# One V load on the SyncE queue: ahead of a transposing DMA instead of behind it

## The chip, the core and the metric

The kernel runs on one core of a Trainium2 chip. Times are device microseconds of one execution. The engines are TensorE (PE, with its weight loads as PEld), VectorE (DVE), ScalarE (ACT), GpSimd (POOL) and SyncE (SP), which here does nothing but issue DMAs.

## The reference

An RWKV-5 attention with a recurrent state, and behind it a feed-forward layer with a SmeLU:

```python
for t in range(S):                      # B, H, S, D = 4, 8, 768, 48
    cur = einsum('bhd,bhe->bhde', u[None] * k[:, :, t], v[:, :, t])
    y[:, :, t] = einsum('bhd,bhde->bhe', r[:, :, t], state + cur)
    state = w[None, :, :, None] * state + einsum('bhd,bhe->bhde', k[:, :, t], v[:, :, t])
x = y.transpose(0, 2, 1, 3).reshape(B * S, H * D)      # 3072 x 384
h = x @ w_in                                           # 384 x 2048
g = where(h >= 1, h, where(h <= -1, 0, (h + 1) ** 2 / 4))
out = g @ w_out                                        # 2048 x 384
```

## The kernel before

The recurrence is worked in chunks of 128 positions. A group is one chunk of two batches; there are 6 chunks by 2 pairs of batches, so 12 groups, numbered 0 to 11. A unit is one batch of a group (group 4 has units 8 and 9). For each group the kernel loads R, K and V in f32 (384 KB each), scales them by powers of w into bf16 (Rs, Ks), transposes these, forms the masked product A of the chunk, multiplies it with V and adds the part from the state: that is y, 128 x 768 in bf16. Its transposed copy xT is the operand of the feed-forward layer, which is worked in four quarters of d_ff: m (matmuls into hp), r, s, g (the SmeLU) and M (matmuls into op), then the copy to o and the store.

The order of all instructions is written out by hand in the table `ORDER`: one word per step, run from left to right, so each engine gets its own steps in that order, and within a queue nothing overtakes. A word is the step's name, the group or unit, `=V`, `=A` or `=G` for the engine and `/` with PSUM banks. Words used below:

- `LR4`, `LK4`, `LV4`: the load of R, K, V of group 4, in `load`, line 253, all issued from SP.
- `V4`: the cast of V32 to bf16 on ScalarE (line 112). The f32 V tiles (`Vi`) have three buffers; loads come in the order LV0, LV1, LV2, LV3, LV5, LV4, LV6, so LV4 writes the buffer that V2 has read.
- `Ks5`, `Rs5`, `KU5`, `RKU5`: scaled products of K and R (line 282), on GpSimd from group 2 on.
- `KT4`, `RT4`: the transposing DMAs of Ks and Rs of group 4 (line 318), from group 4 on, issued from SP.
- `Y8`, `Y9`, `yg4`: the matmuls of y of group 4 (lines 432 and 438), and the addition on VectorE (line 450).
- `xcg3`: the transposing DMA of y of group 3, the fourth group (line 467), from group 3 on, issued from SP.
- `m3.0` to `m3.3`: the four quarters' first matmuls of group 3 (line 475); they read xT. `M3.00` and so on are the second matmuls (line 512).

SP thus carries, in one order, the loads, three kinds of transposing DMAs and the stores. A waiting instruction on SP holds all that stand behind it, also those that wait for nothing.

Of the kernel before, what the change touches and what calls it, by code (L numbers as in the profile page):

```python
# [32 lines left out]
M0.01 g1.0 M1.00/3 M1.10 M1.11 M1.01 Rs2=G s1.2=A g1.2 T5/0 RKU2=G LK4 r1.3=A s1.3=A g1.3 T4/1 LV3 Ks3=G M0.02 M0.03  # L33
LR4 us2 c5=V A5/0 KU3=G Rs3=G c4=V A4/1 AT5 sbf1=A M1.02 M0.12 M0.13 AT4 T6/0 sbf0=A V2 Y4/1 Y5 B2=G og0=A T7/2 c6=A
RKU3=G c7=A yg2 LV5 M1.12 Sp4/0 Sp5 M1.03 X5/2 Tmg2 decayg2=G X4/1 M1.13 A6/0 xc4=A xc5=V m2.0/2 A7/1 us3 AT6 m2.1/0
og1=A LK5 LR5 V3 Y6/3 B3=G sbfg2=A r2.0=A AT7 Y7 m2.2/1 s2.0=A Ks4=G yg3 xcg3 m2.3/3 g2.0 Rs4=G r2.1=A s2.1=A g2.1 LV4
r2.2=A s2.2=A KT4 M2.00/2 M2.10 M2.01 M2.11 r2.3=A KU4=G RT4 RKU4=G g2.2 s2.3=A LK6 m3.0/0 us4 M2.02 m3.1/1 LR6 M2.12
LV6 r3.0 s3.0=A Ks5=G g2.3 M2.03 Sp6/3 Sp7 M2.13 g3.0 m3.2/0 Rs5=G Tmg3 r3.1 s3.1=A RT5 og2=A g3.1 V4 AA4/23 AT9 Ks6=G
r3.2 s3.2=A KT5 m3.3/1 M3.00/3 M3.10 V5 B4=G AT8 Y8/2 Y9 r3.3 g3.2 s3.3=A LK8 M3.11 M3.12 M3.01 M3.02 yg4 AA5/20 g3.3
# [571 lines left out]
```

## Time and profile before

| | us |
|---|---|
| median of three runs | 175.05 (174.41 to 175.17) |
| the profiled execution, its own time | 174.45 |
| its span | 172.7 |
| TensorE's granted clock | 1.0 |

The profile's rows are read like this: a row of the timeline has the start (us from the span's start), the duration, the engine (SPq for SyncE), the line, the operation, what it writes and reads, and how many instructions are merged; a bracket at the end is the engine's idle time before it and what ended it. A DMA's row is only its issue; the time from the start of its issue to its landing stands in the view of DMA issues. The chain of work that ended last is followed back from the last instruction: at each step to what released it, or to the instruction before it on its engine. Matmuls are pipelined and their ends are modelled, so neighbouring rows of TensorE overlap a little.

### The profile page before, as it was taken

The numbers are of one execution on the slowest core, as the hardware profiler recorded it, in microseconds if no ns is written. First come the engines' busy times: TensorE is split into PE (matmuls) and PEld (weight loads), VectorE is DVE, ScalarE is ACT, GpSimd is POOL, SyncE is SP. The second block draws the span as 40 slices with busy tenths as digits, with TensorE's granted clock in tenths as the row PEclk, the third lists the DMA queues.
The fourth block names the chain that finished last, engine by engine and source line by source line (L and its number), as shares of the span: only waits on it lengthen the run. The fifth ranks groups of instructions, "written<-read, shape, count | busy, mean of one in ns | idle before, by whom it ended". The sixth has DMA issues, their size and how long they took to land.

```text
span 172.7 us, 4051 instructions
## 1 busy us (share of the span) xinstructions
PE 164.6 (95%) x1674; PEld 132.8 (77%) x1674; DVE 130.5 (76%) x150; ACT 129.8 (75%) x150; POOL 117.6 (68%) x86
## 2 busy tenths in 40 slices
PE   7989969999999999989999999999999999999991
PEld 5769859866888877588787797696897787888871
DVE  4578798988687788859789779885889958873752
ACT  4355688991699899179979878689695896988940
POOL 3496754998589949999999998999568804300000
PEclk9999999999999999999999999999999999999999
DMA  5999999999995999999999997997999025130022
GB/s 109 193 187 189 200 175 192 222 210 207 176 194 88 212 181 162 193 200 139 201 305 220 185 220 167 209 188 143 294 204 249 4 55 143 39 101 0 8 91 91
DMA packets 103751, 28.26 MB, mean 164 GB/s; under 512 B 98866, under 2 KB 102836, under 8 KB 103732
## 3 DMA queue, kind: packets, MB, share of 16 engines
q1 hardware_dynamic: 101824, 24.75, 79.0%
q0 software_dynamic: 1760, 3.15, 9.9%
q8 instruction: 13, 0.21, 0.6%
q10 hardware_dynamic: 148, 0.10, 0.2%
q14 instruction: 6, 0.05, 0.1%
HBM read 20.45 MB, written 4.72 MB: 146 GB/s over the span
## 4 chain that ended last, share of the span: by engine, by line
PE 88%; ACT 4%; DMA 3%; DVE 2%; issue 1%; POOL 0%; ACTq 0%; DVEq 0%
PE hp L475 35%; PE op L512 34%; PE A L370 3%; PE Y L438 3%; DMA xT<-y 3%; PE Y L432 2%; PE z L566 2%; PE Sp L405 2%; ACT pt L486 1%; PE TK L330 1%; PE T L330 1%; ACT TT L112 1%; PE lwp L207 1%; PE wp L233 1%; PE TR L330 1%; PE up L211 1%
## 5 line engine op out<-in xcount | busy, mean ns | idle before, releaser
L475 PE MATMUL hp<-xT,w_in 128*128 128x256 bf16 x576 | 69.3, 273 | 1.3 <-DMA xT<-y 1.0
L512 PE MATMUL op<-w_out,g 128*128 128x384 bf16 (+1 forms) x400 | 68.5, 320 | 0.0
L498 DVE SCALAR_TENSOR_TENSOR g<-sq,hp 128x1024 bf16<-128x1024 bf16 x48 | 57.9, 1215 | 13.4 <-ACT sq L495 13.4
L475 PEld LDWEIGHTS <-w_in 128*128 128x128 bf16 x576 | 61.9, 114 | 4.8 <-issue 1.6
L486 ACT ACTIVATE pt<-hp 128x1024 f32<-128x1024 f32 x46 | 46.9, 1020 | 13.8 <-PE hp L475 13.8
L512 PEld LDWEIGHTS <-g 128*128 128x128 bf16 x400 | 37.5, 98 | 20.4
L495 ACT ACTIVATE sq<-pt 128x1024 bf16<-128x1024 f32 x46 | 48.3, 1057 | 1.2
L379 DVE TENSOR_TENSOR AT<-A,umask 128x1024 bf16<-128x1024 f32 x20 | 23.7, 1220 | 5.2 <-PE A L370 5.2
L282 POOL TENSOR_TENSOR Ks<-Ki,Wdn 128x768 bf16<-128x768 f32 (+1 forms) x12 | 20.3, 1688 | 8.5 <-DMA Ki<-in_k_dram 4.7
L313 POOL TENSOR_TENSOR V<-Vb,diag 128x768 f32<-128x768 bf16 (+1 forms) x14 | 18.1, 1290 | 9.8 <-DVE diag L304 4.3
L282 POOL TENSOR_TENSOR RKU<-Ri,KU 128x768 f32<-128x768 f32 (+1 forms) x13 | 21.2, 1634 | 1.0 <-DVE KU L282 0.6
L282 POOL TENSOR_TENSOR KU<-Ki,u_sb 128x768 f32<-128x768 f32 (+1 forms) x13 | 21.3, 1636 | 0.5 <-DMA Ki<-in_k_dram 0.5
L416 POOL TENSOR_TENSOR state<-Tm,wCm 128x768 f32<-128x768 f32 x8 | 14.6, 1830 | 9.9 <-DVE Tm L413 9.9
L282 POOL TENSOR_TENSOR Rs<-Ri,Wup 128x768 bf16<-128x768 f32 x10 | 18.3, 1826 | 0.1
L112 ACT CAST Vb<-Vi 128x768 bf16<-128x768 f32 (+1 forms) x14 | 10.2, 733 | 5.9 <-DMA Vi<-in_v_dram 5.8
L450 DVE TENSOR_TENSOR y<-Y,V 128x768 bf16<-128x768 f32 x10 | 9.6, 956 | 5.9 <-PE Y L438 3.3
L304 DVE TENSOR_REDUCE diag<-RKU 128x16 f32<-128x768 f32 (+1 forms) x14 | 11.6, 831 | 1.5 <-POOL RKU L282 1.5
L112 ACT CAST state_bf<-state 128x768 bf16<-128x768 f32 (+1 forms) x12 | 8.5, 717 | 4.2 <-POOL state L416 4.2
L112 ACT COPY o<-op 128x768 f32<-128x768 f32 (+1 forms) x9 | 6.7, 748 | 5.8 <-PE op L512 5.6
L438 PE MATMUL Y<-Vb,AT 128*128 128x48 bf16 x192 | 10.4, 186 | 0.4 <-ACT Vb L112 0.4
L413 DVE TENSOR_TENSOR Tm<-Sp,state 128x768 f32<-128x768 f32 x8 | 7.7, 956 | 3.2 <-PE Sp L405 3.2
L438 PEld LDWEIGHTS <-AT 128*128 128x128 bf16 x192 | 9.5, 98 | 0.7 <-issue 0.5
(73 smaller groups left out, 122.9 us busy)
## 6 DMA issues: line engine op xcount, KB each, us to landing
out_dram<-o SPq DMA_DIRECT2D x11, 384.0 KB, 3.7
Ki<-in_k_dram SPq DMA_DIRECT2D x9, 384.0 KB, 6.1
Ri<-in_r_dram SPq DMA_DIRECT2D x9, 384.0 KB, 6.0
Vi<-in_v_dram SPq DMA_DIRECT2D x9, 384.0 KB, 5.3
Ki<-in_k_dram SPq DMA_DIRECT2D x6, 192.0 KB, 4.0
Ri<-in_r_dram SPq DMA_DIRECT2D x6, 192.0 KB, 4.7
Vi<-in_v_dram SPq DMA_DIRECT2D x6, 192.0 KB, 6.2
w_in<-in_moe_w_in_dram POOLq DMA_DIRECT2D x2, 384.0 KB, 7.7
```

Source lines behind the costliest of these rows:

```text
L112: nc.scalar.copy(out, in_) if e == "A" else engines[e].tensor_copy(out, in_)
L282: engines[e].tensor_mul(part(out)[:, :, :, :D], part(a), rep(b, j1 - j0) if len(b.shape) == 3 and b.shape[1] == H else part(b))
L304: nc.vector.tensor_reduce(d[:, hs], tiles["RKU", g][:, hs, :], AX.X, ALU.add)
L313: engines[e].tensor_mul(t[:, hs, :], tiles["V", g][:, hs, :], tiles["diag", g][:, hs].unsqueeze(2).to_broadcast([P, n, D]))
L379: nc.vector.tensor_mul(t.rearrange("p i n t -> p (i n) t"), tiles["A", n].rearrange("p i (n t) -> p (i n) t", t=P), umask.unsqueeze(1).to_ ...
L416: engines[e].tensor_mul(states[g % BP], tiles["Tm", g], flat(wCm).unsqueeze(1).to_broadcast([P, UNITS, DM]))
L438: nc.tensor.matmul(Y[:, h * D : (h + 1) * D], AT[:, i, p, :], V[:, j * H + h, :], start=(c == 0), stop=True, skip_group_check=True,)
L475: nc.tensor.matmul(hp[:, f, :], w_in_sb[wi][:, i, wo * FG * P + f : (wo + 1) * FG * P : FG], tiles["xT", g][:, :, i, :], start=(i == 0), s ...
L486: nc.scalar.activation(t, tiles["hp", g, q], AF.Relu, bias=0.5, scale=0.5)
L495: nc.scalar.activation(t, p, AF.Square)
L498: nc.vector.scalar_tensor_tensor(out=make("g", ("g", g, q), [P, FG, TOK], BF16), in0=tiles["sq", g, q], scalar=1.0, in1=tiles["hp", g, q], ...
L512: nc.tensor.matmul(tiles[key][:, i, : o1 - o0], tiles["g", g, q][:, f, j * P : (j + 1) * P], w_out_sb[wi][:, wo, f * DO + o0 : f * DO + o1 ...
```

## The change

The word `LV4` moves from behind `g2.1` to ahead of `xcg3`:

```diff
-og1=A LK5 LR5 V3 Y6/3 B3=G sbfg2=A r2.0=A AT7 Y7 m2.2/1 s2.0=A Ks4=G yg3 xcg3 m2.3/3 g2.0 Rs4=G r2.1=A s2.1=A g2.1 LV4
+og1=A LK5 LR5 V3 Y6/3 B3=G sbfg2=A r2.0=A AT7 Y7 m2.2/1 s2.0=A Ks4=G yg3 LV4 xcg3 m2.3/3 g2.0 Rs4=G r2.1=A s2.1=A g2.1
```

Of the words between the two places only `xcg3` is on SP. Here is SyncE's program around that place, with the semaphores that each instruction waits for; the loads at the top are LK5 and LR5, the two transposing DMAs at the bottom KT4 and RT4:

```order
 L253 DMA Ki<-in_k_dram 128x16x48 [waits DMAHW2_49,Pool_49]
 L253 DMA Ri<-in_r_dram 128x16x48 [waits DMAHW3_49,Pool_49]
-L467 DMA_TRANSPOSE xT<-y 128x6x128 [waits DMAHW4_49,DVE_49]
-L253 DMA Vi<-in_v_dram 128x16x48 [waits DMAHW5_49,Activation_49]
+L253 DMA Vi<-in_v_dram 128x16x48 [waits DMAHW5_49,DMAHW4_49,Activation_49]
+L467 DMA_TRANSPOSE xT<-y 128x6x128 [waits DVE_49]
 L318 DMA_TRANSPOSE KT<-Ks 128x8x128 [waits DMAHW6_49,Pool_49]
 L318 DMA_TRANSPOSE RT<-Rs 128x8x128 [waits DMAHW7_49,Pool_49]
```

The two instructions change places. Both take the next of eight DMA semaphores in turn, so they also exchange these; the V load's waits are for earlier DMAs of those semaphores (the halves of V of group 2, which used the same buffer) and for the cast V2.

What stands further behind on SyncE reads the same before and after. These rows are LV6, RT5, KT5, LK8, then the transposing DMA of y of group 4 (xcg4):

```order
L253 DMA Vi<-in_v_dram 128x16x48 [waits DMAHW2_49,Activation_49]
L318 DMA_TRANSPOSE RT<-Rs 128x8x128 [waits DMAHW3_49,Pool_49]
L318 DMA_TRANSPOSE KT<-Ks 128x8x128 [waits DMAHW4_49]
L253 DMA Ki<-in_k_dram 128x16x48 [waits DMAHW5_49]
L467 DMA_TRANSPOSE xT<-y 128x6x128 [waits DMAHW6_49,DVE_49]
```

Nothing moved there; xcg4 is the transposing DMA whose reader is m4.0. TensorE, VectorE, ScalarE and GpSimd keep their programs; only the names of the two exchanged semaphores change in their waits.

## The prediction

> **What bounds the kernel now.** I read the busy times first, then the same by stage, then TensorE's waits, then the chain of work that ended last, and last the rows of the SyncE queue (SP), which the change touches.
>
> ```profile
> span 172.7 us, 4051 instructions
> PE 164.6 (95%) x1674; PEld 132.8 (77%) x1674; DVE 130.5 (76%) x150; ACT 129.8 (75%) x150; POOL 117.6 (68%) x86
> ```
>
> TensorE is the busiest engine by 30 us. The view by stretches says where its idle time lies; its columns are the stretch, its length, and the busy time of PE, PEld, DVE, ACT and POOL.
>
> ```profile
> 54.00:74.00 20.00, 19.16 (x186) 14.23 (x185) 16.36 (x16) 15.49 (x18) 17.47 (x11) 1.00 1.04 176
> 74.00:90.00 16.00, 15.84 (x179) 13.45 (x179) 12.03 (x12) 13.72 (x16) 15.67 (x10) 1.00 1.08 207
> 90.00:164.00 74.00, 74.00 (x747) 60.12 (x745) 57.98 (x55) 61.73 (x66) 45.74 (x27) 1.00 0.74 145
> ```
>
> From 54 to 164 us TensorE idles 0.84 + 0.16 + 0.00 = 1.00 us. TensorE's waits in that stretch are a single row:
>
> ```profile
> PE hp L475 <- DMA xT<-y: 1.0, 1, 1.0
> ```
>
> So behind 54 us one wait, and only that one, can be taken away; after it TensorE runs without a hole to 164 us. The chain shows what it waits for:
>
> ```profile
> 68.71 0.96 DVE y L450
> 69.74 4.38 DMA xT<-y
> 74.16 1.47 PE hp L475 x12
> ```
>
> This is the transposing DMA of the fifth group's y (xcg4): y is done at 68.71 + 0.96 = 69.67, the DMA is issued at 69.74 and lands 4.38 us later, and the first matmul of m4.0 follows at 74.16.
>
> **Why that DMA takes 4.38 us.** The SP queue's rows (start, duration of the issue):
>
> ```profile
> 44.00 1.53 SPq L253 DMA_DIRECT2D Vi<-in_v_dram  x1
> 45.62 1.91 SPq L253 DMA_DIRECT2D Ki<-in_k_dram  x1
> 47.63 2.13 SPq L253 DMA_DIRECT2D Ri<-in_r_dram  x1
> 53.52 1.30 SPq L467 DMA_TRANSPOSE xT<-y  x1
> 54.91 0.53 SPq L253 DMA_DIRECT2D Vi<-in_v_dram  x1
> 55.54 2.48 SPq L318 DMA_TRANSPOSE KT<-Ks  x1
> 58.11 1.26 SPq L318 DMA_TRANSPOSE RT<-Rs  x1
> 59.42 0.58 SPq L253 DMA_DIRECT2D Ki<-in_k_dram  x1
> ...
> 61.61 1.91 SPq L253 DMA_DIRECT2D Vi<-in_v_dram  x1
> 63.62 4.05 SPq L318 DMA_TRANSPOSE RT<-Rs  x1
> 67.71 1.30 SPq L318 DMA_TRANSPOSE KT<-Ks  x1
> 69.07 0.57 SPq L253 DMA_DIRECT2D Ki<-in_k_dram  x1
> 69.74 2.30 SPq L467 DMA_TRANSPOSE xT<-y  x1
> ```
>
> SP stands still from 47.63 + 2.13 = 49.76 to 53.52, waiting for the fourth group's y, and then issues back to back until 72 us. The DMA view gives the times from issue to landing. First the V load at 44.00; then the R load at 47.63, the V load at 54.91 (the one that moves), xcg3 and KT4; then the K load at 69.07, RT5, KT5 and xcg4.
>
> ```profile
> Vi<-in_v_dram SPq DMA_DIRECT2D x1, 384.0 KB, 6.2
> ```
> ```profile
> Ri<-in_r_dram SPq DMA_DIRECT2D x1, 384.0 KB, 6.7
> Vi<-in_v_dram SPq DMA_DIRECT2D x1, 384.0 KB, 4.2
> xT<-y SPq DMA_TRANSPOSE x1, 2.9
> KT<-Ks SPq DMA_TRANSPOSE x1, 4.4
> ```
> ```profile
> Ki<-in_k_dram SPq DMA_DIRECT2D x1, 384.0 KB, 4.3
> RT<-Rs SPq DMA_TRANSPOSE x1, 6.0
> KT<-Ks SPq DMA_TRANSPOSE x1, 2.8
> xT<-y SPq DMA_TRANSPOSE x1, 4.4
> ```
>
> A transposing DMA on an empty queue lands after 2.8 to 2.9 us and its issue takes 1.3; behind loads it takes 4.4 to 6.0, and the issue 2.3 to 4.05. xcg4 stands behind a load issued at 69.07 that itself stands behind everything since 54.91. Meanwhile the DMA engines were idle. These are the shares of 40 slices of 0.25 us from 48 to 58:
>
> ```profile
> DMA  9999999999999999996220000007999115999999
> ```
>
> The hole runs from about 52.6 to 54.7 us: the loads of the fifth group's K and sixth group's R have drained, and SP may not issue what stands behind xcg3.
>
> **The change, part by part.** It moves one instruction, the 384 KB V load (LV4), on one queue; no engine's program is reordered and nothing is added.
>
> *LV4 earlier.* Its buffer is the third group's, whose cast on ScalarE is long done:
>
> ```profile
> 41.56 0.83 ACT L112 CAST Vb<-Vi 128x768 bf16<-128x768 f32 x1 [2.96 <-DMA Vi<-in_v_dram]
> ```
>
> So it is issued at 49.8, for about 2 us like the three loads ahead of it (1.53 to 2.13): SP is free again at 51.9, before y is done. The landings give a load's time on a full queue: 44.00 + 6.2 = 50.2 and 47.63 + 6.7 = 54.3, with two loads' data between: 2.05 us each. LV4 lands at 54.3 + 2.05 = 56.35 instead of 54.91 + 4.2 = 59.1. Nobody waits for it there; its own gain is nothing.
>
> *xcg3 now stands behind a load.* It is issued at 53.52 as before (y sets that). From below it lands at 53.52 + 2.9 = 56.4, as on an empty queue; from above at 53.52 + 6.0 = 59.5, by RT5's row, behind three loads. The nearer rows are those behind one load: the load at 54.91 lands at 59.1 and KT4 at 55.54 + 4.4 = 59.95; the load at 69.07 lands at 73.4 and xcg4 at 74.1. That is 0.7 to 0.85 behind the load, so xcg3 lands at 56.35 + 0.8 = 57.15. Its reader is m3.0:
>
> ```profile
> 54.90 2.76 PE L512 MATMUL op<-w_out,g 128*128 128x384 bf16 x16
> 57.50 1.25 PE L475 MATMUL hp<-xT,w_in 128*128 128x256 bf16 x10
> ```
>
> M2 covers it until 57.50. Cost nothing, with 0.35 us to spare; what goes beyond that is paid in full.
>
> *SP's rows behind it come earlier.* A transposing DMA that stands behind loads lands 1.9 to 2.1 us after its issue ends (KT4: 58.02 to 59.95; RT5: 67.67 to 69.6; xcg4: 72.04 to 74.1). So xcg3's issue ends at about 55.15, and KT4 follows directly, now with no load ahead of it: 1.30, like KT5 behind RT5, instead of 2.48. RT4 adds 1.26 and ends at about 57.8 instead of 59.37. **SP's lead is 1.6 us.** The two loads behind keep it. RT5 also needs Rs5 from GpSimd, and the K load feeds GpSimd's next step:
>
> ```profile
> 60.29 1.82 POOL L282 TENSOR_TENSOR Rs<-Ri,Wup 128x768 bf16<-128x768 f32 x1
> 64.48 1.83 POOL L282 TENSOR_TENSOR Ks<-Ki,Wdn 128x768 bf16<-128x768 f32 x1 [2.38 <-DMA Ki<-in_k_dram]
> ```
>
> Rs5 is done at 62.11, RT5 was issued at 63.62; 1.6 earlier would be 62.0, so that it starts some 0.1 later than the lead allows. That costs nothing, since its 4.05 us are set by the loads draining ahead of it, not by its start: it ends at 66.05. GpSimd's 2.38 us of waiting shrink too, so it falls behind nowhere. KT5 and LK8 follow; LK8 lands at 73.4 - 1.6 = 71.8.
>
> *xcg4.* Still issued at 69.74, because y is set by TensorE. It lands at the later of 69.74 + 2.9 = 72.65 and 71.8 + 0.75 = 72.55. TensorE is ready at 71.69 + 1.48 = 73.17:
>
> ```profile
> 71.69 1.48 PE L512 MATMUL op<-w_out,g 128*128 128x384 bf16 x8
> ```
>
> So the 1.00 us goes entirely, with 0.5 to spare. A lead of 74.1 - 73.17 = 0.95 us is enough for that.
>
> *What is late next.* Behind 74 us the rest moves as one: xcg5 and later ones hang on y, so on TensorE; the loads behind xcg4 are issued about 1 us earlier, since its issue takes 1.30 instead of 2.30; GpSimd has gained more than 1 us; ScalarE waits for TensorE there and can follow:
>
> ```profile
> ACT pt L486 <- PE hp L475: 10.8, 16, 2.1
> ```
>
> **Sum:** 0 (LV4) + 0 (xcg3) - 1.00 (xcg4) = -1.0 us on the profiled execution's own 174.45 us (span 172.7 and 1.75 around it): 173.45. The median of the three runs, 175.05, lies 0.60 above that execution; I take 1.0 off it: **174.05 us**.
>
> **The rivals.**
>
> *The gain comes in part* (174.2 to 174.9, say 174.4). One DMA engine can lag: the shares above fall at 52.6, yet the R load lands at 54.3. RT5, which meets such a lag, ends its issue 0.5 to 0.9 us later than a clean queue would let it. If xcg3 does so, it lands at about 57.7, m3.0 is 0.2 late, and SP's lead is 1.05, just enough: -0.8, 174.25. A lead under 0.95 leaves the difference as a wait. For it: the margins are 0.35 and 0.5 us. Against: each needs tenths beyond my middle. The Trainium skill, "DMA: Bandwidth & Descriptors", section "Queues, rings and completion order", speaks on this side: each DMA engine takes its descriptors in ring order, and a DMA counts as complete only when every engine's part is; the trace agrees (0.8 us behind the load ahead), and by that rule the lag passes on to xcg3.
>
> *The gain is given back* (up to 175.05). TensorE might not be the bound behind 74 us, and catch up with another engine. ScalarE's waits speak against it (10.8 us for TensorE), and so do 74.00 busy of 74.00. The Trainium skill, "Trainium Kernel Development and Optimization", section "Performance Expectations", warns that matmul busy time is a bad metric since matmuls are pipelined, and points to the weight loads: those are busy 60.12 of 74.00 here, which would leave room; the trace's single wait says otherwise, and no run here settles it.
>
> *The change doesn't do what it says* (175.05): LV4 held by its buffer or semaphore until 53.5. The cast at 41.56 and the standing SP speak against it.
>
> *Slower.* xcg3 behind LV4 behaves as RT5 behind three loads: 6.0 us, landing at 59.5, so m3.0 starts 2.0 late. SP is then held for 4.05, to 57.57, and RT4 ends 0.8 later than before. xcg4's wait vanishes under the delay: 2.0 - 1.0 = +1.0, 176.05. It decides from a landing of 58.5 on. For it: R's and K's data are still in flight when LV4 is issued. Against: 3.7 us pass from LV4's issue to xcg3's, against 2.0 between the V load at 61.61 and RT5.
>
> *More than forecast* (173.45): two of three runs took 0.6 to 0.7 us more than the profiled one; if that is a longer wait at the same place, it goes too.
>
> **How the numbers follow.** Forecast 0.50, in part 0.25, given back 0.08, no effect 0.04, slower 0.05, more 0.08. Likeliest: 174.05. The range reaches from "more" to no change with a spread of the runs, 173.4 to 175.1, and leaves out the slower case and the tails. A measurement can tell about 0.5%, 0.88 us, from no change: faster means under 174.17. The forecast lies 0.12 beyond that, so I count 0.40 of its 0.50, all of "more" and a little of "in part": faster 0.50, same 0.45, slower 0.05.
>
> **What would show it.** LV4's issue at 49.8 and its landing near 56.3; xcg3's landing near 57.1 and no wait at m3.0; KT4's issue near 55.2 at 1.3 us; RT4's end near 57.8; GpSimd's wait for K well under 2.38; xcg4's issue at 69.7 with a landing under 73.2; TensorE busy 20.0 of 20.0 from 54 to 74. I am wrong if m3.0 waits for xT, if xcg4 still lands behind 73.2, or if TensorE shows a new wait behind 74.

## The result, and the profile after

| | before | the change |
|---|---|---|
| median of 21 runs each, us | 174.51 (174.03 to 175.81) | 173.41 (173.23 to 175.23) |
| span of the profiled execution, us | 172.7 | 171.5 |

The ratio is 0.9939, with a 95% interval of 0.9920 to 0.9958: faster by 0.6%. In a second, shorter measurement (below) it was 0.9968, 0.9940 to 0.9995. All ratios in this text leave out the few slow runs.

The same stretches as before the change, now of the profile after; the columns are the stretch, its length, and the busy time of PE, PEld, DVE, ACT and POOL:

```profile
54.00:74.00 20.00, 20.00 (x196) 15.16 (x194) 16.29 (x16) 16.28 (x18) 18.61 (x12) 1.00 1.19 187
74.00:90.00 16.00, 16.00 (x183) 13.62 (x181) 13.24 (x13) 14.10 (x15) 15.59 (x10) 1.00 1.00 220
90.00:163.00 73.00, 73.00 (x738) 59.10 (x736) 56.97 (x54) 60.78 (x65) 44.66 (x26) 1.00 0.74 141
```

TensorE is busy for 109.00 of 109.00 us: the hole of 1.00 us is gone, and none has opened behind it. TensorE's timeline after the change, at the first matmuls of m3.0 and of m4.0:

```profile
57.50 1.47 PE L475 MATMUL hp<-xT,w_in 128*128 128x256 bf16 x12
73.00 1.47 PE L475 MATMUL hp<-xT,w_in 128*128 128x256 bf16 x12
```

m3.0 starts where it did before (57.50), m4.0 at 73.00 instead of 74.16. That is 1.16 of the 1.2 us by which the spans differ. The SyncE queue after the change (start, duration of the issue):

```profile
50.05 2.99 SPq L253 DMA_DIRECT2D Vi<-in_v_dram  x1
53.46 1.95 SPq L467 DMA_TRANSPOSE xT<-y  x1
55.51 1.25 SPq L318 DMA_TRANSPOSE KT<-Ks  x1
56.85 1.26 SPq L318 DMA_TRANSPOSE RT<-Rs  x1
...
62.07 3.05 SPq L318 DMA_TRANSPOSE RT<-Rs  x1
65.18 2.40 SPq L318 DMA_TRANSPOSE KT<-Ks  x1
67.63 0.57 SPq L253 DMA_DIRECT2D Ki<-in_k_dram  x1
69.69 1.21 SPq L467 DMA_TRANSPOSE xT<-y  x1
```

LV4 stands in SP's idle time; KT4's issue takes 1.25 instead of 2.48, as no load stands between it and xcg3; and xcg4's takes 1.21 instead of 2.30. The queue is not empty then: LK8, the load ahead of xcg4, lands only at 71.97. But LK8 was issued 2.06 us ahead of xcg4 instead of 0.67, and xcg4 lands 0.63 behind it. The times from issue to landing, in the DMA view of the change: first LV4 and xcg3, then xcg4.

```profile
Vi<-in_v_dram SPq DMA_DIRECT2D x1, 384.0 KB, 6.8
xT<-y SPq DMA_TRANSPOSE x1, 4.0
```
```profile
xT<-y SPq DMA_TRANSPOSE x1, 2.9
```

xcg3 now lands at 53.46 + 4.0 = 57.46, just when m3.0 starts; xcg4 lands at 72.60 instead of 74.12. The DMA engines' busy shares from 48 to 58 us after the change, in slices of 0.25 us, to be laid beside the row shown before:

```profile
DMA  9999999999999999999942149999999994799993
```

The hole of 2 us is filled, but for four slices from 53.0 to 54.0 us, in which the shares are 4, 2, 1 and 4 tenths: together some 0.7 us of idle time.

### The profile page after: what moved, and what is told of

Same layout as the page of the kernel before. It is cut to its first block, busy times and chain, and to the rows that moved or that the text cites. A ratio compares the mean times of both kernels' runs of the same rounds, so it can differ in the third digit from the quotient of the medians.

```text
span 171.5 us, 4050 instructions
## 1 busy us (share of the span) xinstructions
PE 163.4 (95%) x1674; PEld 131.6 (77%) x1674; DVE 130.7 (76%) x150; ACT 130.0 (76%) x150; POOL 117.7 (69%) x86
## 4 chain that ended last, share of the span: by engine, by line
PE 83%; SPq 4%; ACT 3%; DMA 3%; POOL 2%; DVE 1%; issue 1%; POOLq 0%
PE op L512 37%; PE hp L475 36%; SPq L253 4%; PE A L370 3%; DMA Vi<-in_v_dram 3%; PE Y L438 2%; PE Y L432 2%; PE Sp L405 2%; ACT pt L486 1%; ACT Vb L112 1%; POOL V L313 1%; PE T L330 1%; DVE g L498 1%; POOL RKU L282 1%; POOL Ks L282 1%
```

## The experiments

Three theories stood against each other. **Queue**: the gain comes from what no longer stands ahead of xcg4, since a load was moved into the idle time ahead of xcg3. **V**: it comes from V being there earlier. **Given back**: what is gained at one place is lost further on. The first four kernels were measured together beside before, and so were the next three. Before was profiled only once, with the first measurement; its median was 174.51 us there, 174.19 beside the first four and 174.57 beside the next three. So starts and spans can be compared with those of before only to some tenths of a microsecond. Whether a matmul waits is seen within each trace.

**The same amount in the queue, V early.** On top of the change, LR7 is put where LV4 stood:

```diff
-... yg3 LV4 xcg3 m2.3/3 ... g2.1 r2.2=A ... m4.0/1 LR7 KU5=G
+... yg3 LV4 xcg3 m2.3/3 ... g2.1 LR7 r2.2=A ... m4.0/1 KU5=G
```

> The change, with the R load of group 7 (LR7, 384 KB, until now right behind xcg4) put where LV4 stood, behind xcg3. V of group 4 stays early, but as much is queued between xcg3 and xcg4 as before the change. Queue theory: SP's lead is gone, KT4's issue ends near 58.0 to 58.4 again, xcg4 lands near 74.1 to 74.5, m4.0 waits 1.0 to 1.4 us, ratio to before 0.999 to 1.003. V theory (the gain comes from V being there earlier, through its cast, GpSimd's product and the state): the gain stays, ratio 0.994.

Measured: ratio 1.0037 (1.0021 to 1.0054), a little above the expected 0.999 to 1.003. SP's rows (KT4, then xcg4) and TensorE's row of m4.0 in this kernel's timeline:

```profile
55.50 2.69 SPq L318 DMA_TRANSPOSE KT<-Ks  x1
...
70.01 2.10 SPq L467 DMA_TRANSPOSE xT<-y  x1
```
```profile
74.24 0.93 PE L475 MATMUL hp<-xT,w_in 128*128 128x256 bf16 x7 [1.12 <-DMA xT<-y]
```

V is as early as in the change (issued at 49.33), and the wait is back with 1.12 us. The V theory falls.

**Another load in the hole.** Before, with LK6 in the place that the change gives to LV4:

```diff
-... yg3 xcg3 m2.3/3 ... s2.3=A LK6 m3.0/0
+... yg3 LK6 xcg3 m2.3/3 ... s2.3=A m3.0/0
```

> Before, with the K load of group 6 (LK6) ahead of xcg3 instead of LV4, which stays behind xcg3. Queue theory: any load of this size that fills the hole does the same: xcg3 lands near 57.4, xcg4 near 72.6 to 73.0, m4.0 doesn't wait, ratio 0.993 to 0.995. V theory: V comes no earlier than before, so no gain, ratio 1.000.

Measured: ratio 0.9980 (0.9954 to 1.0005); the medians are 173.53 and 174.19. m3.0 and m4.0 in its timeline:

```profile
57.65 1.47 PE L475 MATMUL hp<-xT,w_in 128*128 128x256 bf16 x12
...
73.15 1.47 PE L475 MATMUL hp<-xT,w_in 128*128 128x256 bf16 x12
```

In the profile it does what the change does: m4.0 1.01 us earlier with no wait, m3.0 0.15 late, span 171.7. The ratio points the same way, but it lies outside the expected 0.993 to 0.995 and its interval holds 1, the V theory's value. So by time alone this is not settled; only the trace, in which the wait is gone, speaks here for the queue theory.

**Only the wait at m4.0.** Before, with LK8, the load right ahead of xcg4, put right behind it:

```diff
-... s3.3=A LK8 M3.11 ... M3.03 xcg4 m4.0/1
+... s3.3=A M3.11 ... M3.03 xcg4 LK8 m4.0/1
```

> Before, with the K load that stands right ahead of xcg4 (LK8) put right behind it; nothing moves at xcg3. Queue theory: xcg4 is issued at 69.74 on a queue that has drained since KT5 (issue end 69.01), lands near 72.6 to 72.9, m4.0 starts near 73.0, ratio 0.993 to 0.994: the whole gain without touching LV4. V theory: no gain, ratio 1.000. If something behind m4.0 depended on the loads coming earlier, the ratio lies between.

Measured: ratio 1.0017 (0.9995 to 1.0039): no gain, a miss. By the ratio alone this is the V theory's value, so the trace has to tell. Its SP queue, and TensorE's rows of m4.0 and of m5's first quarter:

```profile
69.64 1.21 SPq L467 DMA_TRANSPOSE xT<-y  x1
70.90 0.57 SPq L253 DMA_DIRECT2D Ki<-in_k_dram  x1
71.53 1.53 SPq L253 DMA_DIRECT2D Ri<-in_r_dram  x1
73.11 1.74 SPq L253 DMA_DIRECT2D Ki<-in_k_dram  x1
74.94 3.45 SPq L253 DMA_DIRECT2D Vi<-in_v_dram  x1
78.49 2.12 SPq L467 DMA_TRANSPOSE xT<-y  x1
```
```profile
72.95 1.47 PE L475 MATMUL hp<-xT,w_in 128*128 128x256 bf16 x12
...
82.86 1.47 PE L475 MATMUL hp<-xT,w_in 128*128 128x256 bf16 x12 [0.81 <-DMA xT<-y]
```

m4.0 behaves as expected: 1.2 us earlier, no wait. But xcg5 now stands behind four loads instead of three: y of group 5 is done at 77.86, xcg5 is issued at 78.49 and its issue ends at 80.61, and m5 waits 0.81 us. So the wait was not removed but handed on. m5 still starts 0.23 us earlier than before (83.09 there); of that 0.03 are left at 89.69, and at 96.08 the kernel is 0.14 late, with no further wait of TensorE that the profile lists. This is the "given back" theory, for this kernel, and the queue is what takes the gain back.

**Two loads in the hole**, the prediction's slower case: the change, and LK6 as well ahead of xcg3.

```diff
-... yg3 LV4 xcg3 m2.3/3 ... s2.3=A LK6 m3.0/0
+... yg3 LV4 LK6 xcg3 m2.3/3 ... s2.3=A m3.0/0
```

> The change, and LK6 as well ahead of xcg3: two loads in the hole. The prediction's slower case, measured: LK6's issue lasts until about 54.5 to 55, xcg3's issue starts late and lands about 2 us later than with one load, near 59.5, so that m3.0 waits 1.9 to 2.1 us; m4.0 doesn't wait. Net +0.8 to +1.0 us, ratio 1.004 to 1.006. If the queue's order did not matter for xcg3 (its data going ahead of the loads'), xcg3 would land near 57.4 and the ratio be 0.993 to 0.994.

Measured: ratio 1.0052 (1.0026 to 1.0078). Its SP queue, and TensorE at m3.0 and m4.0:

```profile
49.62 2.38 SPq L253 DMA_DIRECT2D Vi<-in_v_dram  x1
52.05 1.76 SPq L253 DMA_DIRECT2D Ki<-in_k_dram  x1
53.91 2.77 SPq L467 DMA_TRANSPOSE xT<-y  x1
```
```profile
58.72 1.47 PE L475 MATMUL hp<-xT,w_in 128*128 128x256 bf16 x12 [0.98 <-DMA xT<-y]
...
74.22 1.04 PE L475 MATMUL hp<-xT,w_in 128*128 128x256 bf16 x8
```

The direction and the ratio are as expected, the size at m3.0 is not: 1.2 us late, not 2.0, since xcg3 lands at 58.7 and not at 59.5. The span is 0.1 us longer than before's; beside the median of before timed with it (174.19), its profiled 174.53 us are 0.34 longer. The timed runs are longer by 0.5%, and what takes the rest the one profile doesn't show.

**Half the load.** LV4 as two halves, one on each side of xcg3:

```diff
-... yg3 xcg3 m2.3/3 ... g2.1 LV4
+... yg3 LV4.0 xcg3 m2.3/3 ... g2.1 LV4.1
```

> LV4 as two halves of 192 KB, the first ahead of xcg3, the second behind it. Queue theory, by its size: xcg3 lands near 56.6 and m3.0 is not late; KT4's issue ends near 57.0 instead of 58.0, the lead is 0.7 to 1.0, xcg4 lands near 73.1 to 73.5 and m4.0 starts at 73.1 to 73.6: ratio 0.994 to 0.997. If it were all or nothing: 1.000.

Measured: ratio 0.9974 (0.9953 to 0.9994). m4.0:

```profile
73.90 1.36 PE L475 MATMUL hp<-xT,w_in 128*128 128x256 bf16 x11 [0.79 <-DMA xT<-y]
```

xcg3 landed at 56.60 and m3.0 was not late, as expected; KT4's issue ended at 57.42, a lead of 0.6 us. xcg4 landed at 73.86, so 0.26 us were gained and 0.79 of the wait stayed: part of the gain, less of it than expected (m4.0 at 73.1 to 73.6). The lead shrank on the way: KT5's issue ends at 68.73 instead of 69.01, which leaves 0.28.

**The change, and LK8 behind xcg4.** The miss above left two readings of the queue theory:

```diff
-... yg3 LV4 xcg3 m2.3/3 ... s3.3=A LK8 M3.11 ... M3.03 xcg4 m4.0/1
+... yg3 LV4 xcg3 m2.3/3 ... s3.3=A M3.11 ... M3.03 xcg4 LK8 m4.0/1
```

> The change, and LK8 behind xcg4 as well. LK8 behind xcg4 alone took the wait away at m4.0 and got 0.8 us of it back one group later, at m5, where xcg5 stood behind four loads instead of three. If what counts is only what stands between one y and the next (theory A): four loads again, xcg5 lands near 82.7, m5 waits 0.8 to 1.0, ratio 0.999 to 1.001, the change's gain lost. If filling the hole shortens the queue for good (theory B): the lead reaches xcg5, no wait at m5, ratio 0.993 to 0.994.

Measured: ratio 1.0029 (0.9998 to 1.0059), above the expected 0.999 to 1.001, which the interval still touches. m5's first quarter:

```profile
82.92 1.47 PE L475 MATMUL hp<-xT,w_in 128*128 128x256 bf16 x12 [0.88 <-DMA xT<-y]
```

Theory A: with four loads between xcg4 and xcg5 the wait at m5 is there, though the hole was filled. The change's gain is lost; the profiled span of 173.1 us is even 0.4 above before's, and the wait at m5 alone doesn't explain that.

**The change once more**, beside these two:

> The change as it is, beside the next two on one chip. Queue theory: as in its first measurement, ratio to before 0.992 to 0.996; m4.0 starts near 73.0 and m3.0 is 0.0 to 0.2 us late. If the first measurement owed something to its chip: nearer to the run with LK6 in the hole, 0.998.

Measured: ratio 0.9968 (0.9940 to 0.9995).

```profile
57.62 1.47 PE L475 MATMUL hp<-xT,w_in 128*128 128x256 bf16 x12
...
73.12 1.47 PE L475 MATMUL hp<-xT,w_in 128*128 128x256 bf16 x12
```

m4.0 1.04 us earlier, m3.0 0.12 late. The intervals of the two measurements overlap from 0.9940 to 0.9958, so they don't contradict each other. But 0.9968 lies just outside the expected 0.992 to 0.996, nearer to the 0.998 of the run with LK6 than to the first 0.9939. That there is a gain is shown twice; the two intervals together leave its size in timed runs between 0.05% and 0.8%.

**What the seven runs say together.** What counts is what SP must move from one y to the next. The following count was made after the runs and is an estimate: a load is taken at the 2.05 us that it needs on a full queue, a transposing DMA at its issue of 1.3. From xcg3's issue to xcg4's there are 16.2 us (53.52 to 69.74). Before, they held five loads (LV4, LK6, LR6, LV6, LK8), four transposing DMAs and xcg3's own: 10.25 + 5.2 + 1.3 = 16.75, more than fits, so xcg4 stands behind a load that was issued only just ahead of it. With four loads it is 14.7, which fits. From xcg4's issue to y of group 5 there are 8.2 us in the run with LK8 moved (69.64 to 77.86); three loads and xcg4's own make 7.45 and fit, four make 9.5 and don't. Ahead of xcg3 SP stands still for 3.7 us: one load fits, two (4.1) don't. The change moves the one load that had too much ahead of it into the one stretch that had too little.

The count gives the direction, not the size, and one run goes against it. The kernel with half the load has four and a half loads between the two, 15.7 us, which should fit; yet 0.79 us of its wait stayed. Why its lead shrank on the way to xcg4, where that of the change held, no run shows. Nor do the runs tell whether the time of the DMA engines or the held issues of SP are the limit; a V load on another queue might tell, and was not run.

## Why the prediction was right

Forecast was 1.0 us (0.57%); measured are 0.61% by the ratio and 1.16 us in the profile. The mechanism is the one forecast: the wait at m4.0 goes because xcg4 finds less ahead of it, and the runs above show that this, and not V, is the cause. The time itself came out by luck. The forecast of 174.05 us was built on the median of three runs; the median of before in 21 runs is 0.54 lower, so the time came out at 173.41, 0.01 above the range's lower end, with the ratio as forecast.

- **LV4 earlier.** Issued at 50.05 (forecast 49.8). Its issue took 2.99 us, not 2; it lands at 56.83, not 56.35. Two loads were outstanding, and the issue ended at 53.04, just when the DMA engines' shares fell: this is what is left of the hole.
- **xcg3 behind a load.** Landing 57.46 (forecast 57.15), 0.63 behind LV4. The spare 0.35 us were all used up. M2 ahead of it ran 0.07 us earlier than in the old profile, and m3.0 started at the same 57.50, so 0.07 us were paid; by the same reckoning 0.19 in the second profile (54.83 and 57.62). Cost nothing was right only nearly. The Trainium skill, "DMA: Bandwidth & Descriptors", section "Queues, rings and completion order", says that each DMA engine takes its descriptors in ring order. The runs agree: xcg3 lands at 56.60 behind half a load, 57.46 behind one, 58.68 behind two.
- **SP's lead.** RT4's issue ends at 58.11 instead of 59.37: 1.26, not 1.6. The missing 0.3 us is xcg3's later landing.
- **RT5, KT5, LK8.** RT5 starts at 62.07 (forecast 62.1, set by Rs5) and ends at 65.12, not 66.05; KT5 takes 2.40, not 1.30. The two errors cancel: LK8 is issued at 67.63 (forecast 67.5). The prediction put the whole hold on RT5; it is shared by the two, and their sum is steadier: KT5's issue ends at 67.58 here, at 67.61 in the change's second profile and at 67.53 with LK8 moved as well, where RT5 took 3.80 and KT5 1.30.
- **xcg4.** Issued at 69.69, landing 72.60 (forecast 72.65), wait gone.
- **The size of the wait.** This is the term of the sum that was mis-sized: 1.00 by the wait row, 1.16 by m4.0's start. The row counts from the modelled end of the matmul before (73.17), while the next may start at 73.00 already, as it does now. The start of the waiting instruction, not the idle time ahead of it, was the number to take.
- **What is late next.** Nothing, in the change: TensorE's first matmuls behind m4.0 all start 1.15 to 1.17 us earlier, to the last of them (161.28 instead of 162.45). The Trainium skill, "Trainium Kernel Development and Optimization", section "Performance Expectations", calls matmul busy time a bad metric for how close a kernel is to roofline. That is another question than whether a gain is passed on. One of the prediction's rivals was that the room in PEld (59.10 of 73.00) might swallow the gain. It didn't here: where the trace shows no wait of TensorE at all, its time was worth its full length.
- **A slip.** The prediction calls the loads at 45.62 and 47.63 the fifth group's K and the sixth group's R; both are of the sixth group (LK5, LR5). Nothing hangs on it.
- **GpSimd** was to fall behind nowhere; it waits less at Ks6, 0.94 instead of 2.38 us:

```profile
62.98 1.83 POOL L282 TENSOR_TENSOR Ks<-Ki,Wdn 128x768 bf16<-128x768 f32 x1 [0.94 <-PE Sp L405]
```

**The rivals.** "Slower" was a sound mechanism: it needed a second load to come true, and its turning point was forecast at a landing of 58.5; with 58.68 the profiled execution stands 0.1 us over before. "In part" is what half the load does. "Given back" did not happen to the change, but to both kernels with LK8 behind xcg4, and there by the queue, not by another engine catching up as that rival had it. "The change doesn't do what it says" falls with LV4's issue at 50.05. "More than forecast" named 173.45, and 173.41 was measured, but not for its reason: the median of before, 174.51, is close to the 174.45 of its profiled execution, so there was no longer wait to take away.

## What to carry to other kernels

When an in-order DMA queue stands idle at an instruction that waits for a result, look for a later load that waits for nothing and fits into that idle time, and move just that one; count what then stands between each result and the next against the time between them. A load moved behind the late transfer instead of ahead of the previous one made the next transfer late here. And take the gain from the waiting instruction's start, not from the idle time shown ahead of it.

## What was unexpected of the hardware

LV4's issue behind two outstanding loads took 2.99 us, against 0.53 before the change, behind a transposing DMA alone, and the DMA engines' shares were low for 1 us before its data began. LV7 behind three loads took 3.45 (with LK8 moved behind xcg4). The number of loads ahead doesn't settle it: LV7 behind the same LR7 and LK7 took 1.94 before the change and 3.20 after it. What sets it no run here shows.

Transposing DMAs behind loads are held in the same way (1.21 to 1.32 without, up to 4.20 with loads ahead), and not only while the loads' data move. KT5's issue in the change ends at 67.58, but the DMA engines stand all but idle from 66.7 to 67.7 us. These are their shares from 62.1 to 69.8, in 40 slices:

```profile
DMA  9999999999999999999999580000069999999679
```

RT5, right ahead of KT5, lands at 68.89, 2.2 us behind the end of that busy stretch.

A landing can lie well behind the end of most of the data in other cases too: before the change the shares fell at 52.6 and the R load landed at 54.3. In the DMA view of before from 48 to 58 us stands one packet of another queue (its columns: packets, MB, share of 16 engines):

```profile
q8 instruction: 1, 0.02, 0.9%
```

0.9% of 16 engines over 10 us is 1.4 us of one engine, about the size of the lag. That this fetch of instructions held up that engine's part of the load fits, but was not tested.
